# A planner with same-engine latencies, and attention scores on two 64-column array tiles, in a two-layer recurrent-attention kernel

## The chip, the cores and the metric

One core of a Trainium2 chip. The metric is the device time of one execution, in microseconds (us). Engines are named as in the profile: PE (TensorE matmuls), PEld (its weight loads), DVE (VectorE), ACT (ScalarE), POOL, SP.

## The reference, cut to what matters

Two equal layers, each recurrent memory attention followed by a gated feed-forward. Attention runs over 64 segments of 32 tokens; 8 memory rows go from each segment to the next, so a segment can't start before the one before it has gone through Wo.

```python
for s in range(n_seg):                      # 64 segments
    h = concat([mem, x[:, s*32:(s+1)*32]])  # 40 rows, 512 wide
    q, k, v = h@Wq, h@Wk, h@Wv              # 32 heads of 128
    p = softmax(where(mask, q@k.T * scale, -1e9))   # 40 x 40 per head
    o = (p@v) @ Wo
    mem = o[:, :8]; outs.append(o[:, 8:])
...
x = x + A(layernorm(x)); x = x + B(layernorm(x))    # layer 1
x = x + A(layernorm(x)); x = x + B(layernorm(x))    # layer 2
```

## The kernel before

Layer 2 runs six segments behind layer 1, so that a step (70 in all, 58 of them with both layers) handles one segment of each: 80 columns in place of 40. Layer 1 sits in partitions 0 to 39, layer 2 in 64 to 103. Nothing is issued where it is written: every piece of work goes to a planner as a task with an engine, an estimated duration and what it reads and writes. The planner (a list scheduler, longest remaining path first) fixes the order, which then stands in the program. The planner's numbers thus never are the time; they only decide the order.

```python
LAT = {"PE": 215.0, "DVE": 130.0, "ACT": 140.0, "POOL": 450.0, "SP": 2200.0}
...
for tk in reversed(T):                     # length of the remaining path
    m = 0.0
    for s in tk.succ:
        same = T[s].eng == tk.eng
        m = max(m, T[s].tail + (0.0 if same else tk.lat))   # same engine: no latency
    tk.tail = m + tk.dur + tk.boost
```

The score matmuls of a unit of three heads, and the softmax chain that follows each group of six heads:

```python
for i in range(nh):
    for idx, j in enumerate(jobs):         # j = layer; the unused half of lhsT holds zeros
        nc.tensor.matmul(s_all[:, uh - h0 + i, :], lhsT=qku[:, i, j, :],
                         rhs=qku[:, i, 2 + j, JOFF*j : JOFF*j + L],
                         start=(idx == 0), stop=(idx == len(jobs) - 1))
# ... then, per group:
# DVE  st = s_ps + mask          (L410)   reads the one score bank
# DVE  mx = max(st)              (L413)
# DVE  st = st - mx              (L415)
# ACT  st = exp(scale * st)      (L418)
# DVE  sm = sum(st)              (L420)
# DVE  rs = 1 / sm               (L422)
# DVE  pb = st * rs, per layer   (L426)   partitions 0.. and 64..
# PE   transpose pb into pt_ps   (L436)
```

Of the kernel before, what the change touches and what calls it, by code (L numbers as in the profile page):

```python
# [12 lines left out]
ALU = mybir.AluOpType  # L13
# [6 lines left out]
L = MEM + SEG  # L20
JOFF = 64
LW = JOFF + L
BLK = 4
EPS = 1e-5
# [16 lines left out]


class Task:
    __slots__ = ("eng", "dur", "lat", "fn", "deps", "succ", "tail", "boost", "ndep", "ready", "start", "idx", "on")

    def __init__(self, eng, dur, lat, fn, boost):
        self.eng, self.dur, self.lat, self.fn, self.boost = eng, dur, lat, fn, boost
        self.deps, self.succ = set(), []


class Planner:



    LAT = {"PE": 215.0, "DVE": 130.0, "ACT": 140.0, "POOL": 450.0, "SP": 2200.0}

    def __init__(self):
        self.tasks = []
# [3 lines left out]
    def add(self, eng, dur, fn, r=(), w=(), lat=None, boost=0.0):  # L62
        engs = eng if isinstance(eng, tuple) else (eng,)
        tk = Task(engs, dur, self.LAT[engs[0]] if lat is None else lat, fn, boost)
        tk.idx = len(self.tasks)
        for k in r:
            if k in self.writer:
                tk.deps.add(self.writer[k])
        for k in w:
            if k in self.writer:  # L70
                tk.deps.add(self.writer[k])
            for q in self.readers.get(k, ()):
                tk.deps.add(q)
        for k in w:
            self.writer[k] = tk.idx
            self.readers[k] = []
        for k in r:
            self.readers.setdefault(k, []).append(tk.idx)
        tk.deps.discard(tk.idx)
        self.tasks.append(tk)  # L80
        return tk

    def plan(self):
        T = self.tasks
        for tk in T:
            for d in tk.deps:
                T[d].succ.append(tk.idx)
        for tk in reversed(T):
            m = 0.0
            for s in tk.succ:  # L90
                same = T[s].eng == tk.eng
                m = max(m, T[s].tail + (0.0 if same else tk.lat))
            tk.tail = m + tk.dur + tk.boost
        free, avail = {"PE": 0.0, "ACT": 0.0}, {"PE": [], "ACT": []}
        for tk in T:
            tk.ndep = len(tk.deps)
            tk.ready = 0.0
            for e in tk.eng:
                free.setdefault(e, 0.0)
                avail.setdefault(e, [])  # L100
        waiting = {e: [] for e in free}
        ready = {e: [] for e in free}

        def release(tk):
            for e in tk.eng:
                heapq.heappush(waiting[e], (tk.ready, tk.idx))

        for tk in T:
            tk.on = None
            if tk.ndep == 0:  # L110
                release(tk)
        order = []
        left = len(T)
        while left:
            best = None
            for e in free:
                q, h = waiting[e], ready[e]
                while h and T[h[0][1]].on is not None:
                    heapq.heappop(h)
                while q and T[q[0][1]].on is not None:  # L120
                    heapq.heappop(q)
                if h:
                    t = free[e]
                elif q:
                    t = max(free[e], q[0][0])
                else:
                    continue
                if best is None or t < best[0]:
                    best = (t, e)
            t, e = best  # L130
            q, h = waiting[e], ready[e]
            while q and q[0][0] <= t:
                _, i = heapq.heappop(q)
                if T[i].on is None:
                    heapq.heappush(h, (-T[i].tail, i))
            while T[h[0][1]].on is not None:
                heapq.heappop(h)
            tk = T[heapq.heappop(h)[1]]
            tk.on, tk.start = e, t
            free[e] = t + tk.dur  # L140
            order.append(tk)
            left -= 1
            for s in tk.succ:
                n = T[s]
                same = n.eng == (e,)
                n.ready = max(n.ready, t + tk.dur + (0.0 if same else tk.lat))
                n.ndep -= 1
                if n.ndep == 0:
                    release(n)
        self.span = max(free.values())  # L150
        order.sort(key=lambda k: (k.start, k.idx))
        return order


class Kern:
# [149 lines left out]
    def layernorm_T(self, xb, xkey):  # L305
        nc, pl, D, DC = self.nc, self.pl, self.D, self.DC
        i = self.nxt("lns", 3)
        ln = self.lns[i]
        lk = ("lns", i)
        xi = self.nxt("xn", len(self.xn))  # L310
        xn = self.xn[xi]
        pl.add("DVE", dve_ns(D), lambda: nc.vector.bn_stats(out=ln[:, 0:6], in_=xb), r=[xkey], w=[lk])
        pl.add("DVE", 100, lambda: nc.vector.bn_aggr(out=ln[:, 6:8], in_=ln[:, 0:6]), w=[lk])
        pl.add("DVE", 80, lambda: nc.vector.tensor_scalar(out=ln[:, 8:9], in0=ln[:, 7:8], scalar1=EPS, scalar2=None, op0=ALU.add), w=[lk])
        pl.add("POOL", 500, lambda: nc.gpsimd.tensor_tensor(out=ln[:, 9:10], in0=ln[:, 8:9], in1=self.negh[:], op=ALU.pow), w=[lk], lat=100)
        pl.add("DVE", 80, lambda: nc.vector.scalar_tensor_tensor(out=ln[:, 10:11], in0=ln[:, 6:7], scalar=-1.0, in1=ln[:, 9:10],
                                                                  op0=ALU.mult, op1=ALU.mult), w=[lk])
        pl.add("ACT", act_ns(D) + 180, lambda: nc.scalar.activation(out=xn[:], in_=xb, func=ACTF.Identity, bias=ln[:, 10:11], scale=ln[:, 9:10]),
               r=[xkey, lk], w=[("xn", xi)])
        pst = self.misc[:, 0:(DC * P) // 2].bitcast(BF16).rearrange("p (c n) -> p c n", c=DC)  # L320

        def tr():
            for c in range(DC):
                nc.tensor.transpose(out=pst[:, c, :], in_=xn[:, c * P:(c + 1) * P], identity=self.ident[:])

        pl.add("PE", DC * mm_ns(P), tr, r=[("xn", xi)], w=["misc"])
        return pst
# [18 lines left out]
    def emit_step(self, t):  # L346
        nc, pl = self.nc, self.pl
        DC, H, LAG, R = self.DC, self.H, self.LAG, self.R
        jobs = tuple(j for j in (0, 1) if 0 <= t - j * LAG < self.NSEG)
# [15 lines left out]
        s_all = self.s_ps[:, 0:6 * L].rearrange("p (h k) -> p h k", h=6)  # L365
        pt_all = self.pt_ps[:, 0:6 * 2 * L].rearrange("p (h k) -> p h k", k=2 * L)

        for g, (h0, gsz, us) in enumerate(self.groups):
            hs = slice(0, gsz)
            for u in us:  # L370
                uh, nh = self.units[u]
# [3 lines left out]
                qku = self.qku[qi]  # L375

                def qk(uh=uh, nh=nh, pq=pq):
                    for i in range(nh):
# [10 lines left out]
                       w=[("pj", pji)])  # L389
# [10 lines left out]
                def sc(uh=uh, nh=nh, qku=qku, h0=h0):  # L400
                    for i in range(nh):
                        for idx, j in enumerate(jobs):
                            nc.tensor.matmul(s_all[:, uh - h0 + i, :], lhsT=qku[:, i, j, :], rhs=qku[:, i, 2 + j, JOFF * j:JOFF * j + L],  # L403
                                             start=(idx == 0), stop=(idx == len(jobs) - 1))

                pl.add("PE", nh * len(jobs) * mm_ns(L), sc, r=[("qku", qi)], w=["s_ps"])
            gi = self.nxt("st", 2)
            st, pb, mx, sm, rs = self.st[gi], self.pb[gi], self.mx[gi], self.sm[gi], self.rs[gi]
            n = gsz * L
            pl.add("DVE", dve_ns(n, True), lambda gsz=gsz, hs=hs, st=st: nc.vector.tensor_tensor(  # L410
                out=st[pr, hs], in0=s_all[pr, hs], in1=self.maskb[pr, :].unsqueeze(1).to_broadcast([npart, gsz, L]), op=ALU.add),
                r=["s_ps"], w=[("st", gi)])
            pl.add("DVE", dve_ns(n), lambda hs=hs, st=st, mx=mx: nc.vector.tensor_reduce(out=mx[pr, hs], in_=st[pr, hs], axis=AX.X, op=ALU.max),  # L413
                   r=[("st", gi)], w=[("mx", gi)])
            pl.add("DVE", dve_ns(n), lambda gsz=gsz, hs=hs, st=st, mx=mx: nc.vector.tensor_tensor(  # L415
                out=st[pr, hs], in0=st[pr, hs], in1=mx[pr, hs].unsqueeze(2).to_broadcast([npart, gsz, L]), op=ALU.subtract),
                r=[("mx", gi)], w=[("st", gi)])
            pl.add("ACT", act_ns(n), lambda hs=hs, st=st: nc.scalar.activation(out=st[pr, hs], in_=st[pr, hs], func=ACTF.Exp, scale=self.scale),  # L418
                   w=[("st", gi)])
            pl.add("DVE", dve_ns(n), lambda hs=hs, st=st, sm=sm: nc.vector.tensor_reduce(out=sm[pr, hs], in_=st[pr, hs], axis=AX.X, op=ALU.add),  # L420
                   r=[("st", gi)], w=[("sm", gi)])
            pl.add("DVE", 110, lambda hs=hs, rs=rs, sm=sm: nc.vector.reciprocal(out=rs[pr, hs], in_=sm[pr, hs]), r=[("sm", gi)], w=[("rs", gi)])  # L422
            for j in jobs:
# [3 lines left out]
                    out=pb[pj_, hs, JOFF * j:JOFF * j + L], in0=st[pj_, hs],  # L427
                    in1=rs[pj_, hs].unsqueeze(2).to_broadcast([npj_, gsz, L]), op=ALU.mult), r=[("st", gi), ("rs", gi)], w=[("pb", gi, j)])
# [14 lines left out]
            for n0 in range(0, H, 4):  # L443
# [5 lines left out]
                def vmm(pv=pv, n0=n0):  # L449
                    for c in range(DC):  # L450
# [5 lines left out]
                       r=[("pj", pji)], w=[("vsb", n0 // 4)])  # L456
# [38 lines left out]
        for idx, j in enumerate(jobs):  # L495
            s = t - j * LAG
            b = s // BLK
# [161 lines left out]
```

## Time and profile before

| | before |
|---|---|
| median of its first 3 runs | 2194.81 us |
| profiled span | 2196.4 us |
| matmuls, all with their own weight load | 42,116 |
| score matmuls (40 columns) | 4,096 |

The lines below are from the groups of instructions of the kernel before. The columns are: line, engine, operation, output and inputs, shape, count; then busy us and mean ns of one; then idle us of the engine just before them and what ended most of it.

```profile
L403 PE MATMUL s_ps<-qku 128*128 128x40 bf16 x4096 | 201.6, 180 | 24.5 <-DVE st L410 21.7
L403 PEld LDWEIGHTS <-qku 128*128 128x128 bf16 x4096 | 173.1, 96 | 78.6 <-issue 34.5
L436 PE MATMUL pt_ps<-ident,pb 128*128 128x80 bf16 (+1 forms) x2240 | 145.4, 198 | 32.8 <-DVE pb L426 27.8
```

A matmul's 180 ns here is a modelled life in a pipeline, not what it costs PE; the cost is how soon the next one starts, 25 ns. The last column shows where PE really stood still: at the scores until the bank was read, at the transposition until pb came.

### The profile page before, as it was taken

Reading aid. Unit: us, or ns where it says so; the run is one execution under the profiler, and the core shown is the slowest. Engines: PE = TensorE matmul, PEld = TensorE weight load, DVE = VectorE, ACT = ScalarE, POOL = GpSimd, SP = SyncE. Lnnn points to the kernel's source line nnn. Section 1 sums busy time; section 2 is a strip of 40 time slices with the busy share of each in tenths; the row PEclk is TensorE's granted clock in tenths of the full one; section 3 lists DMA queues with packets and bytes.
Section 4 is the critical chain, followed back from the end, with each engine's and each line's share of the span. In section 5 each row is a group of like instructions: output and inputs, shape, how many; then the busy total and the mean of one; then the engine's idle time right before and its main releaser. Section 6 shows DMA issues by size and latency. Waiting matters only on the chain.

```text
span 2196.4 us, 93329 instructions
## 1 busy us (share of the span) xinstructions
PE 2056.8 (94%) x42116; PEld 1742.8 (79%) x42116; DVE 1270.8 (58%) x3743; ACT 1299.0 (59%) x2919; POOL 43.5 (2%) x77
## 2 busy tenths in 40 slices
PE   4999999999999999999999999999999999999996
PEld 3777878788887878888787778878787888878775
DVE  4566566556646655665566466556655655565653
ACT  3556566565656656565666556566665666666552
POOL 1000000000000000000000000000000000000000
PEclk8999999999999999999999999999999999999997
DMA  9030223233232323324132332423233242324223
GB/s 333 29 89 17 77 60 108 74 108 103 75 108 60 108 74 108 103 75 122 55 113 60 108 103 74 119 58 109 63 113 98 83 116 60 115 58 126 70 61 107
DMA packets 317330, 203.17 MB, mean 92 GB/s; under 512 B 11770, under 2 KB 316930, under 8 KB 316930
## 3 DMA queue, kind: packets, MB, share of 16 engines
q1 hardware_dynamic: 316930, 197.19, 30.7%
q8 instruction: 329, 5.39, 1.0%
q14 instruction: 71, 0.58, 0.1%
HBM read 195.04 MB, written 2.10 MB: 90 GB/s over the span
## 4 chain that ended last, share of the span: by engine, by line
PE 62%; DVE 29%; issue 3%; ACT 3%; DMA 2%; POOL 0%; DVEq 0%; POOLq 0%; ACTq 0%
PE pj L385 22%; PE pj L451 16%; PE misc_ps L535 7%; PE wo_ps L477 7%; DVE pb L426 7%; DVE st L410 4%; DVE mx L413 3%; DVE st L415 3%; DVE sm L420 3%; PE misc_ps L556 3%; PE s_ps L403 3%; DVE ptsb L601 2%; DMA wd<-in_B_w_down_dram 2%; PE ot_ps L461 2%; PE pt_ps L436 2%
## 5 line engine op out<-in xcount | busy, mean ns | idle before, releaser
L385 PE MATMUL pj<-hT,wq_sb 128*128 128x80 bf16 (+1 forms) x8960 | 626.4, 198 | 16.1 <-DVE hT L488 13.6
L385 PE MATMUL pj<-hT,wk_sb 128*128 128x80 bf16 (+1 forms) x8960 | 627.6, 198 | 0.0
L451 PE MATMUL pj<-wv_sb,hT 128*104 128x512 bf16 x2240 | 568.3, 384 | 1.8 <-ACT vsb L599 1.6
L385 PEld LDWEIGHTS <-wq_sb 128*128 128x128 bf16 x8960 | 465.2, 99 | 59.6 <-issue 21.7
L599 ACT CAST qku<-pj 128x480 bf16<-128x480 f32 (+3 forms) x770 | 389.4, 514 | 144.4 <-PE pj L385 103.9
L599 ACT CAST vsb<-pj 104x512 bf16<-104x512 f32 (+2 forms) x560 | 326.1, 585 | 229.4 <-PE pj L451 223.4
L385 PEld LDWEIGHTS <-wk_sb 128*128 128x128 bf16 x8960 | 451.1, 99 | 0.0
L477 PE MATMUL wo_ps<-otsb,wo_sb 128*128 128x80 bf16 (+1 forms) x8960 | 389.3, 198 | 4.6 <-ACT otsb L599 4.2
L477 PEld LDWEIGHTS <-wo_sb 128*128 128x128 bf16 x8960 | 351.2, 99 | 40.7 <-issue 9.3
L451 PEld LDWEIGHTS <-hT 128*104 128x104 bf16 x2240 | 253.3, 128 | 128.1 <-issue 5.1
L410 DVE TENSOR_TENSOR st<-s_ps,maskb 104x240 f32<-104x240 f32 (+5 forms) x420 | 158.0, 376 | 296.7 <-PE s_ps L403 290.0
L426 DVE TENSOR_TENSOR pb<-st,rs 64x240 bf16<-64x240 f32 (+3 forms) x768 | 287.9, 375 | 26.7 <-DVE rs L422 0.5
L418 ACT ACTIVATE st<-st 104x240 f32<-104x240 f32 (+5 forms) x420 | 161.2, 384 | 188.2 <-DVE st L415 185.7
L599 ACT CAST otsb<-ot_ps 128x480 bf16<-128x480 f32 (+3 forms) x420 | 204.4, 487 | 66.6 <-PE ot_ps L461 60.4
L403 PEld LDWEIGHTS <-qku 128*128 128x128 bf16 x4096 | 173.1, 96 | 78.6 <-issue 34.5
L403 PE MATMUL s_ps<-qku 128*128 128x40 bf16 x4096 | 201.6, 180 | 24.5 <-DVE st L410 21.7
L544 DVE SCALAR_TENSOR_TENSOR hff<-th,misc_ps 128x256 bf16<-128x256 f32 x224 | 93.4, 417 | 210.6 <-ACT th L542 208.9
L420 DVE TENSOR_REDUCE sm<-st 104x6 f32<-104x240 f32 (+5 forms) x420 | 155.8, 371 | 95.7 <-ACT st L418 92.9
L535 PE MATMUL misc_ps<-xnT,wg 128*128 128x128 bf16 x1792 | 176.3, 222 | 9.5 <-DVE hff L544 6.6
L535 PE MATMUL misc_ps<-xnT,wu 128*128 128x128 bf16 x1792 | 176.6, 222 | 0.0
L436 PE MATMUL pt_ps<-ident,pb 128*128 128x80 bf16 (+1 forms) x2240 | 145.4, 198 | 32.8 <-DVE pb L426 27.8
L413 DVE TENSOR_REDUCE mx<-st 104x6 f32<-104x240 f32 (+5 forms) x420 | 156.9, 374 | 13.5
(52 smaller groups left out, 1671.3 us busy)
## 6 DMA issues: line engine op xcount, KB each, us to landing
wg<-in_B_w_gate_dram SPq DMA_DIRECT2D x224, 256.0 KB, 3.1
wu<-in_B_w_up_dram SPq DMA_DIRECT2D x224, 256.0 KB, 3.5
wd<-in_B_w_down_dram SPq DMA_DIRECT2D x224, 256.0 KB, 2.9
wv_sb<-in_A_Wv_dram SPq DMA_DIRECT2D x8, 512.0 KB, 9.6
wo_sb<-in_A_Wo_dram SPq DMA_DIRECT2D x8, 512.0 KB, 8.1
wq_sb<-in_A_Wq_dram SPq DMA_DIRECT2D x5, 768.0 KB, 10.3
wk_sb<-in_A_Wk_dram SPq DMA_DIRECT2D x5, 768.0 KB, 11.1
xs<-in_A_x_dram SPq DMA_DIRECT2D x16, 128.0 KB, 2.1
```

What stands on the lines that cost most here:

```text
L385: nc.tensor.matmul(o_ap, lhsT=W[:, c, h * P:(h + 1) * P], rhs=mv(c), start=(c == 0), stop=(c == DC - 1))
L403: nc.tensor.matmul(s_all[:, uh - h0 + i, :], lhsT=qku[:, i, j, :], rhs=qku[:, i, 2 + j, JOFF * j:JOFF * j + L], start=(idx == 0), stop=(id ...
L410: pl.add("DVE", dve_ns(n, True), lambda gsz=gsz, hs=hs, st=st: nc.vector.tensor_tensor(out=st[pr, hs], in0=s_all[pr, hs], in1=self.maskb[p ...
L413: pl.add("DVE", dve_ns(n), lambda hs=hs, st=st, mx=mx: nc.vector.tensor_reduce(out=mx[pr, hs], in_=st[pr, hs], axis=AX.X, op=ALU.max), r=[ ...
L418: pl.add("ACT", act_ns(n), lambda hs=hs, st=st: nc.scalar.activation(out=st[pr, hs], in_=st[pr, hs], func=ACTF.Exp, scale=self.scale), w=[ ...
L420: pl.add("DVE", dve_ns(n), lambda hs=hs, st=st, sm=sm: nc.vector.tensor_reduce(out=sm[pr, hs], in_=st[pr, hs], axis=AX.X, op=ALU.add), r=[ ...
L426: pl.add("DVE", dve_ns(n), lambda gsz=gsz, hs=hs, st=st, rs=rs, pb=pb, pj_=pj_, npj_=npj_, j=j: nc.vector.tensor_tensor(out=pb[pj_, hs, JO ...
L436: nc.tensor.matmul(o_ap, lhsT=pb[:, hl, :], rhs=idn, start=True, stop=True)
L451: nc.tensor.matmul(pv[0:LW, :], lhsT=hT[:, c, :], rhs=self.wv[:, c, n0 * P:(n0 + 4) * P], start=(c == 0), stop=(c == DC - 1))
L477: nc.tensor.matmul(self.wo_ps[:, c * ncol:(c + 1) * ncol], lhsT=self.wo[:, h, c * P:(c + 1) * P], rhs=otsb[:, hl, 0:ncol], start=(h == 0 a ...
L535: nc.tensor.matmul(gu[:, 2 * i + k, :], lhsT=W[:, c, i * P:(i + 1) * P], rhs=xnT[:, c, :], start=(c == 0), stop=(c == DC - 1))
L599: nc.scalar.copy(out=dst, in_=src)
```

## The change

Two parts. The **plan** now charges a latency between two tasks of DVE or of ACT where the second reads what the first has just written, and 45 ns more for any result that PE waits for; its other latencies between engines fall by 8 to 10 ns. The **scores** use one 64-column tile of the array per layer: columns 0 to 63 write partitions 0 to 63, columns 64 to 127 write 64 to 127, each a complete matmul without the zero half. The rest of the diff, cut here, marks which reads are of fresh results, uses `gap` at the second place where the planner had `same`, and plans 520 ns in place of 500 for POOL's one operation.

```diff
-    LAT = {"PE": 215.0, "DVE": 130.0, "ACT": 140.0, "POOL": 450.0, "SP": 2200.0}
+    LAT = {"PE": 205.0, "DVE": 122.0, "ACT": 130.0, "POOL": 100.0, "SP": 2200.0}
+    TO_PE = 45.0
...
+    def gap(self, a, b):
+        if a.eng == b.eng:
+            return a.lat if a.idx in b.fresh and a.eng[0] in ("DVE", "ACT") else 0.0
+        return a.lat + (self.TO_PE if b.eng[0] == "PE" else 0.0)
...
-                m = max(m, T[s].tail + (0.0 if same else tk.lat))
+                m = max(m, T[s].tail + self.gap(tk, T[s]))
...
-                            nc.tensor.matmul(s_all[:, uh - h0 + i, :], lhsT=qku[:, i, j, :], rhs=qku[:, i, 2 + j, JOFF * j:JOFF * j + L],
-                                             start=(idx == 0), stop=(idx == len(jobs) - 1))
+                            js = slice(JOFF * j, JOFF * j + JOFF)
+                            nc.tensor.matmul(s_all[js, uh - h0 + i, :], lhsT=qku[:, i, j, js], rhs=qku[:, i, 2 + j, JOFF * j:JOFF * j + L],
+                                             start=True, stop=True)
```

More of the change, by code (lines that the diff above doesn't have):

```diff
@@ L43 @@
 class Task:
-    __slots__ = ("eng", "dur", "lat", "fn", "deps", "succ", "tail", "boost", "ndep", "ready", "start", "idx", "on")
+    __slots__ = ("eng", "dur", "lat", "fn", "deps", "succ", "tail", "boost", "ndep", "ready", "start", "idx", "on", "fresh")
     def __init__(self, eng, dur, lat, fn, boost):
         self.eng, self.dur, self.lat, self.fn, self.boost = eng, dur, lat, fn, boost
-        self.deps, self.succ = set(), []
+        self.deps, self.succ, self.fresh = set(), [], set()
 class Planner:
-    LAT = {"PE": 215.0, "DVE": 130.0, "ACT": 140.0, "POOL": 450.0, "SP": 2200.0}
+    LAT = {"PE": 205.0, "DVE": 122.0, "ACT": 130.0, "POOL": 100.0, "SP": 2200.0}
+    TO_PE = 45.0
     def __init__(self):
@@ L68, in add @@
                 tk.deps.add(self.writer[k])
+                tk.fresh.add(self.writer[k])
         for k in w:
@@ L90, in plan @@
             for s in tk.succ:
-                same = T[s].eng == tk.eng
-                m = max(m, T[s].tail + (0.0 if same else tk.lat))
+                m = max(m, T[s].tail + self.gap(tk, T[s]))
             tk.tail = m + tk.dur + tk.boost
@@ L144, in plan @@
                 n = T[s]
-                same = n.eng == (e,)
-                n.ready = max(n.ready, t + tk.dur + (0.0 if same else tk.lat))
+                n.ready = max(n.ready, t + tk.dur + self.gap(tk, n))
                 n.ndep -= 1
@@ L312, in layernorm_T @@
         pl.add("DVE", dve_ns(D), lambda: nc.vector.bn_stats(out=ln[:, 0:6], in_=xb), r=[xkey], w=[lk])
-        pl.add("DVE", 100, lambda: nc.vector.bn_aggr(out=ln[:, 6:8], in_=ln[:, 0:6]), w=[lk])
-        pl.add("DVE", 80, lambda: nc.vector.tensor_scalar(out=ln[:, 8:9], in0=ln[:, 7:8], scalar1=EPS, scalar2=None, op0=ALU.add), w=[lk])
-        pl.add("POOL", 500, lambda: nc.gpsimd.tensor_tensor(out=ln[:, 9:10], in0=ln[:, 8:9], in1=self.negh[:], op=ALU.pow), w=[lk], lat=100)
+        pl.add("DVE", 100, lambda: nc.vector.bn_aggr(out=ln[:, 6:8], in_=ln[:, 0:6]), r=[lk], w=[lk])
+        pl.add("DVE", 80, lambda: nc.vector.tensor_scalar(out=ln[:, 8:9], in0=ln[:, 7:8], scalar1=EPS, scalar2=None, op0=ALU.add), r=[lk], w=[lk])
+        pl.add("POOL", 520, lambda: nc.gpsimd.tensor_tensor(out=ln[:, 9:10], in0=ln[:, 8:9], in1=self.negh[:], op=ALU.pow), r=[lk], w=[lk])
         pl.add("DVE", 80, lambda: nc.vector.scalar_tensor_tensor(out=ln[:, 10:11], in0=ln[:, 6:7], scalar=-1.0, in1=ln[:, 9:10],
-                                                                  op0=ALU.mult, op1=ALU.mult), w=[lk])
+                                                                  op0=ALU.mult, op1=ALU.mult), r=[lk], w=[lk])
         pl.add("ACT", act_ns(D) + 180, lambda: nc.scalar.activation(out=xn[:], in_=xb, func=ACTF.Identity, bias=ln[:, 10:11], scale=ln[:, 9:10]),
@@ L416, in emit_step @@
                 out=st[pr, hs], in0=st[pr, hs], in1=mx[pr, hs].unsqueeze(2).to_broadcast([npart, gsz, L]), op=ALU.subtract),
-                r=[("mx", gi)], w=[("st", gi)])
+                r=[("mx", gi), ("st", gi)], w=[("st", gi)])
             pl.add("ACT", act_ns(n), lambda hs=hs, st=st: nc.scalar.activation(out=st[pr, hs], in_=st[pr, hs], func=ACTF.Exp, scale=self.scale),
-                   w=[("st", gi)])
+                   r=[("st", gi)], w=[("st", gi)])
             pl.add("DVE", dve_ns(n), lambda hs=hs, st=st, sm=sm: nc.vector.tensor_reduce(out=sm[pr, hs], in_=st[pr, hs], axis=AX.X, op=ALU.add),
```

## The prediction

> **What bounds the kernel now.** I read the page first: busy shares, slices, chain. They name one engine.
>
> ```profile
> PE 2056.8 (94%) x42116; PEld 1742.8 (79%) x42116; DVE 1270.8 (58%) x3743; ACT 1299.0 (59%) x2919; POOL 43.5 (2%) x77
> ...
> PE   4999999999999999999999999999999999999996
> ...
> PEclk8999999999999999999999999999999999999997
> ...
> PE 62%; DVE 29%; issue 3%; ACT 3%; DMA 2%; POOL 0%; DVEq 0%; POOLq 0%; ACTq 0%
> ```
>
> PE is at 90% or more in every slice but the first and last, at a full clock; DVE and ACT are below 60%. But matmul ends are modelled, so 94% does not say that 94% is needed. For that I took the timeline of two short windows and read starts, not durations.
>
> ```profile
> 1001.68 0.31 PE L385 MATMUL pj<-hT,wk_sb 128*128 128x80 bf16 x4
> ...
> 1001.83 0.31 PE L403 MATMUL s_ps<-qku 128*128 128x40 bf16 x6
> ...
> 1001.98 0.30 PE L385 MATMUL pj<-hT,wq_sb 128*128 128x80 bf16 x4
> ...
> 1002.12 0.31 PE L385 MATMUL pj<-hT,wk_sb 128*128 128x80 bf16 x4
> ```
>
> Four 80-column matmuls go by in 0.144 us (36 ns each), six 40-column score matmuls in 0.150 us (25 ns each). Over all individual starts the medians are 36 ns (80 columns), 25 (40), 56 (128) and 216 (512). Counts by shape from the groups of instructions: 25,984 x 35.6 + 9,472 x 25 + 3,968 x 55.6 + 2,688 x 215.6 ns = 926 + 237 + 221 + 580 = 1,963 us of pure streaming. The span is 2,196, so 233 us (10.6%) is not streaming: 9 before the first matmul, 4 after the last one starts, and 215 in spacings longer than the shape needs, of which 194 lie in 400 spacings that are late by 100 ns or more. About 60 of the total sit in the first and last 100 us; between, it is a steady 7 to 8 us in every 100. The waits name who makes PE late:
>
> ```profile
> PE pt_ps L436 <- DVE pb L426: 27.8, 41, 2.9
> ...
> PE s_ps L403 <- DVE st L410: 21.7, 32, 1.1
> ...
> PE misc_ps L324 <- ACT xn L318: 19.3, 17, 3.4
> ...
> PE pj L385 <- DVE hT L488: 13.6, 43, 0.3
> ```
>
> The softmax chain on DVE ends late for the transposition (L436), the score bank is still being read when the next group's scores want it (L403), and each step's first projection waits for the memory rows of the step before (L385). These are waits that a static order can hide or fail to hide. The order is made by a planner in the kernel, and its picture of DVE is wrong here:
>
> ```profile
> 1000.28 0.41 DVE L410 TENSOR_TENSOR st<-s_ps,maskb 104x240 f32<-104x240 f32 x1 [0.51 <-PE s_ps L403]
> ...
> 1000.72 0.40 DVE L413 TENSOR_REDUCE mx<-st 104x6 f32<-104x240 f32 x1
> ...
> 1001.15 0.41 DVE L415 TENSOR_TENSOR st<-st,mx 104x240 f32<-104x240 f32 x1
> ```
>
> Each of these needs the one before it, and they start 0.43 to 0.44 us apart. Where the next DVE instruction is independent (L413 followed by another group's L420) the median spacing is 0.319. The planner before charges 320 ns and nothing for the dependence.
>
> **What the Trainium skill says.** (1) "TensorE: Matmul & The Clock Gate", Part 1: matmuls start N/2.4 + about 2.5 ns apart, never under about 25 ns. The trace agrees: 36, 56, 216 and 25 ns. So the score matmuls stand on a floor, and fewer rows or columns of weights alone make none faster. (2) "TensorEngine Tiling (Array Packing)", Restrictions and Key Properties: column tiling switches fast weight load off, and changing the tiling mode, not just the tile, drains the engine. The kernel before is untiled all through, so its trace shows no drain. It does show a load that is not a full 128 columns wide: V loads 104 columns, and its second matmul starts 236 ns after the first, not 216, when 40-column matmuls went before, 231 after 80-column ones. Such a load takes about 25 + 20 = 45 to 36 + 15 = 51 ns. (3) "TensorE: Matmul & The Clock Gate", Part 3: matmuls on different tiles overlap, about 4 ns apart in start; no run here shows it. (4) "VectorE: DVE Perf Modes", Two Vector instructions with no wait between them: an instruction whose operands start in another quadrant than the last is held. The trace agrees: the two pb writes (L426, partitions 0 and 64) are independent, yet 414 ns apart. Neither planner knows this.
>
> **The change, part by part.**
>
> *The plan.* Nothing is added or removed on any engine: the counts of matmuls by kind are equal, so the 1,963 us stay. What moves is the order. I built both and measured, in streaming time on PE, how much other work the order puts between a producer and its consumer, and compared it with the time the consumer needs. The need is set so that the shortfalls of the kernel before add up to the stall its trace shows there; the same need then goes over the new order.
>
> - Scores to transposition (420 groups): need 3.39 us, stall 49 us. The lowest 5% of distances rises from 2.60 to 3.24: shortfall left 25. Gain 24. This is the 4 x 122 ns of dependence now in the plan, plus 45 to PE.
> - Scores to the next group's scores: need 1.24, stall 35; lowest 5% from 0.88 to 1.10, lowest 10% from 0.88 to 1.32: 7 left. Gain 27.
> - Step to step (69): need 0.50, stall 24; the median filler goes from 0.04 to 0.47: 14 left. Gain 10.
> - Last down-projection to the next transposition (16): need 5.2, filler 4.18 to 4.61: gain 6.
> - PV to Wo: need 0.69, the lowest 5% falls from 0.46 to 0.33: loss 9. PV to PV, transposition to PV and gate-up to gate-up: losses of 5, 2 and 1.
> - Q/K to scores: the low tail shortens (lowest 5% 1.94 to 1.52). Its need cannot be told from the bank's; the cast takes about 1.0 to 1.1 us with its waits, and few lie under that: loss 0 to 10.
>
> Sum: 67 gained, 17 to 27 lost, about 45 us off (2.0%). Shortfalls at several edges overlap, and a new order makes new waits, so I take 10 to 80.
>
> *The score tiles.* 4,096 matmuls and 4,096 loads stay; loads go from 128 fast columns to 64 slow ones. Scaled from V: 64/104 x (45 to 51) = 28 to 31 ns, an estimate. If loads run one behind another, each score matmul takes 28 to 31 in place of 25: +12 to +25 us. If the two layers' tiles truly overlap, a pair takes about 30 in place of 50: 1,856 pairs x 20 = 37 us saved. Entry and exit: in the new order the score matmuls stand in 501 unbroken blocks (624 before), so 1,002 mode changes. A drain in the skill's sense costs at least the 128 rows (53 ns at 2.4 GHz, an estimate from the array in "TensorE: Matmul & The Clock Gate") plus a load that can no longer be hidden (about 30): 1,002 x 85 ns = +85 us, all on PE, none beside anything. Zero padding: the removed half of the weights was multiplied anyway, so no time in it. Dropping the accumulation across layers saves no instruction.
>
> **The rivals.**
>
> 1. *Tiles are nearly free, the plan decides.* For: V shows a slow load in the middle of fast ones with a delay of 15 to 20 ns and no drain. 2,195 - 45 + 5 = 2,155; 2,110 with a good plan and overlapping tiles. I give it 0.55.
> 2. *Each mode change drains.* For: the skill says so. The plan's gain is eaten: 2,195 - 45 + 85 = 2,235. 0.35.
> 3. *The drain is the whole matmul latency* (the records put a 40-column matmul at 179 ns, modelled). 1,002 x 150 ns = +150: 2,300. 0.10.
> 4. *The plan only moves waits.* DVE holds (414 ns pairs) and bank waits stay unmodelled, and the gain falls to 10. That adds 35 to any of the above. DVE as the new bound I rule out at 58% busy; weight DMA, at 3 us to landing and 31% share, too.
>
> **Range and chances.** The median of the mixture lies between rivals 1 and 2, nearer to 1: 2,170 us. Low end 2,110 (rival 1 with everything well), high end 2,255 (rival 2 with a weak plan). Faster by 2% means under 2,151: a little over half of rival 1, 0.36. Slower means over 2,239: rival 3, and a good third of rival 2 less its better plans, 0.20. Within 2%: 0.44.
>
> **What would show it right or wrong.** Plan: the waits of L436-to-pb and L403-to-st (now L443 and L410) should fall together by half, those of Wo on otsb rise by some us. Tiles: the start-to-start spacing inside score blocks (25 now) should be 28 to 31 if loads bound it, about 15 if pairs overlap; the spacing from the last matmul before a score block to its first, and from its last to the next kind, should show 0 or 50 and more beyond the shape's own time, with nothing waited for. A drain near 150 ns, or score spacings of 50 ns, would prove me wrong upward; plan waits that fall to nothing would, downward.

## The result, and the profile after

| | before | after |
|---|---|---|
| median | 2194.74 us (4 runs) | 2168.38 us (4 runs) |
| lowest to highest | 2193.3 to 2200.37 | 2167.15 to 2169.21 |
| profiled span | 2196.4 us | 2167.4 us |

The ratio is 0.9875, with a 95% interval of 0.9857 to 0.9893: the same within 2%, 26 us faster. A ratio here is always the mean time of one kernel's fast runs over that of the other's fast runs of the same rounds, so not quite the ratio of the medians beside it. The kernel before is run anew with each set of rounds; its medians were 2194.7 to 2197.8 us, so kernels of different sets are best compared by their ratios.

These are the lines of the page of the changed kernel that answer to the first ones shown of before: busy time, PE by slices, its clock, the chain that ended last by engine.

```profile
PE 2091.9 (97%) x42006; PEld 1751.3 (81%) x42116; DVE 1204.5 (56%) x3702; ACT 1307.1 (60%) x2960; POOL 43.7 (2%) x77
...
PE   5999999999999999999999999999999999999996
...
PEclk8999999999999999999999999999999999999997
...
PE 92%; DVE 3%; ACT 2%; issue 1%; DMA 1%; another core or an unknown queue 0%; SPq 0%; POOLq 0%; ACTq 0%; DVEq 0%
```

The chain has changed its nature: DVE held 29% of it and holds 3%. PE is busier by 35 us in a span shorter by 29. (110 matmul records are missing from this trace.) The waits of the changed kernel that answer to those of before (columns: who waited for whom, us in total, times, longest us):

```profile
PE pt_ps L443 <- DVE pb L433: 11.6, 7, 2.9
...
PE misc_ps L330 <- ACT xn L324: 7.7, 4, 3.4
...
PE pj L391 <- DVE hT L495: 5.3, 17, 0.3
```

Seven waits for pb in place of 41, and the scores' wait for the bank is not in the list any more. The four waits shown of before sum to 82 us, and these to 25: 58 us less idle PE at four places alone, yet the span fell by 29 only. Where the rest went is seen in the timeline. This is a place in the changed kernel where four score matmuls (two heads, both layers) stand between two blocks of twelve Wo matmuls (columns: start us, us, engine, line, operation, count):

```profile
1007.02 0.59 PE L484 MATMUL wo_ps<-otsb,wo_sb 128*128 128x80 bf16 x12
1007.55 0.24 PE L410 MATMUL s_ps<-qku 128*64 128x40 bf16 x4
1007.72 0.60 PE L484 MATMUL wo_ps<-otsb,wo_sb 128*128 128x80 bf16 x12
```

Read the starts. Twelve Wo matmuls stream in 12 x 36 ns = 0.43 us, but the scores start 0.53 us after the first: 0.10 lost before the block. The four scores then last until 1007.72, 0.17 us, where four at 25 ns need 0.10. PE counts as busy all through, since the modelled ends of its matmuls reach over the hole. The individual starts of the whole trace say it exactly:

| spacing, ns (median) | before | after |
|---|---|---|
| last 80-column matmul to first score | 36 | 132 |
| last 128-column matmul to first score | 56 | 149 |
| last 512-column matmul to first score | 216 | 309 |
| last 40-column matmul of another kind to first score | 25 | 109 |
| last score to the next kind | 25 | 118 |
| inside a block, both layers | 25 each | pairs 3 to 4 apart; second pair 53 after the first, then one pair every 32 |
| inside a block, one layer only | 25 each | 31 to 32 each after the first two |

So going into a block costs 93 to 96 ns beyond the shape's own time (84 after a 40-column matmul, 51 of the 501 blocks), and going out 93 more. Inside a block two matmuls take 32 ns, so 16 each: the prediction had named "about 15 if pairs overlap".

### The profile page after: what moved, and what is told of

Read it like the earlier page. It is cut to its first block, busy times and chain, and to the rows that moved or that the text cites. A ratio compares the mean times of both kernels' runs of the same rounds, so it can differ in the third digit from the quotient of the medians.

```text
span 2167.4 us, 93419 instructions
## 1 busy us (share of the span) xinstructions
PE 2091.9 (97%) x42006; PEld 1751.3 (81%) x42116; DVE 1204.5 (56%) x3702; ACT 1307.1 (60%) x2960; POOL 43.7 (2%) x77
## 4 chain that ended last, share of the span: by engine, by line
PE 92%; DVE 3%; ACT 2%; issue 1%; DMA 1%; another core or an unknown queue 0%; SPq 0%; POOLq 0%; ACTq 0%; DVEq 0%
PE pj L391 28%; PE pj L458 23%; PE wo_ps L484 13%; PE misc_ps L542 10%; PE s_ps L410 6%; PE pt_ps L443 4%; PE ot_ps L468 3%; PE misc_ps L563 3%; DMA wd<-in_B_w_down_dram 1%; PE misc_ps L330 1%; ACT ptsb L606 1%; ACT otsb L606 1%; DVE sm L427 1%; ACT st L425 0%
## 5 line engine op out<-in xcount | busy, mean ns | idle before, releaser
L391 PEld LDWEIGHTS <-wq_sb 128*128 128x128 bf16 x8960 | 471.3, 99 | 71.6 <-issue 13.8
L606 ACT CAST qku<-pj 128x480 bf16<-128x480 f32 (+3 forms) x770 | 380.7, 514 | 208.0 <-PE pj L391 177.3
L484 PE MATMUL wo_ps<-otsb,wo_sb 128*128 128x80 bf16 (+1 forms) x8960 | 397.7, 198 | 10.7 <-ACT otsb L606 9.6
L606 ACT CAST ptsb<-pt_ps 128x480 bf16<-128x480 f32 (+3 forms) x291 | 138.2, 475 | 82.5 <-PE pt_ps L443 78.8
L422 DVE TENSOR_TENSOR st<-st,mx 104x240 f32<-104x240 f32 (+5 forms) x420 | 158.3, 377 | 9.6
L410 PE MATMUL s_ps<-qku 128*64 128x40 bf16 x4096 | 160.9, 191 | 0.9 <-ACT qku L606 0.7
```

Of the source, the lines that this page charges most:

```text
L391: nc.tensor.matmul(o_ap, lhsT=W[:, c, h * P:(h + 1) * P], rhs=mv(c), start=(c == 0), stop=(c == DC - 1))
L410: nc.tensor.matmul(s_all[js, uh - h0 + i, :], lhsT=qku[:, i, j, js], rhs=qku[:, i, 2 + j, JOFF * j:JOFF * j + L], start=True, stop=True)
L422: pl.add("DVE", dve_ns(n), lambda gsz=gsz, hs=hs, st=st, mx=mx: nc.vector.tensor_tensor(out=st[pr, hs], in0=st[pr, hs], in1=mx[pr, hs].uns ...
L484: nc.tensor.matmul(self.wo_ps[:, c * ncol:(c + 1) * ncol], lhsT=self.wo[:, h, c * P:(c + 1) * P], rhs=otsb[:, hl, 0:ncol], start=(h == 0 a ...
L606: nc.scalar.copy(out=dst, in_=src)
```

## The experiments

The two parts of the change are independent: the planner never looks at what a task issues. The order of all instructions in e1 is that of the changed kernel, and in e2 that of the kernel before; the traces agree: the same operations in the same order on DVE, ACT and POOL, and on PE but for the missing records. There were twelve runs, in three sets, of ten different kernels, and all gave correct results.

### The plan alone, the tiles alone (e1, e2)

**e1_plan_only** is the changed kernel with the score matmuls put back:

```diff
-                            js = slice(JOFF * j, JOFF * j + JOFF)
-                            nc.tensor.matmul(s_all[js, ...], lhsT=qku[:, i, j, js], ..., start=True, stop=True)
+                            nc.tensor.matmul(s_all[:, ...], lhsT=qku[:, i, j, :], ..., start=(idx == 0), stop=(idx == len(jobs) - 1))
```

> The new plan with the score matmuls of the kernel before (untiled, zero padded); the order on every engine is that of the changed kernel. Theory A (from the changed kernel's trace): the tiles cost PE about 72 us net (501 blocks x about 190 ns of entry and exit, less about 18 ns per pair), so the plan alone is worth about 98 us: 2,085 to 2,125 us, some of the waits coming back that the mode changes had covered. Theory B (the prediction's own sum): the plan is worth 45 us and the tiles cost about 20: 2,140 to 2,160 us.

Measured: 2103.42 us, ratio 0.9574 (0.9558 to 0.959). Theory A holds, and the prediction's sum (B) falls. The same place in the program in e1's timeline:

```profile
1005.37 0.59 PE L483 MATMUL wo_ps<-otsb,wo_sb 128*128 128x80 bf16 x12
1005.79 0.26 PE L409 MATMUL s_ps<-qku 128*128 128x40 bf16 x4
1005.90 0.59 PE L483 MATMUL wo_ps<-otsb,wo_sb 128*128 128x80 bf16 x12
```

From Wo to the scores 0.42 us, where it was 0.53; the scores 0.11, where they were 0.17. And e1's waits are about those of the changed kernel (the first two lines are busy time and the chain that ended last):

```profile
PE 2026.0 (96%) x42116; PEld 1734.5 (83%) x42116; DVE 1196.4 (57%) x3702; ACT 1302.9 (62%) x2960; POOL 43.7 (2%) x77
...
PE 86%; DVE 8%; ACT 3%; issue 1%; DMA 1%; POOL 0%; ACTq 0%; POOLq 0%; DVEq 0%
...
PE pt_ps L442 <- DVE pb L432: 12.4, 7, 2.9
...
PE misc_ps L330 <- ACT xn L324: 10.5, 17, 3.4
```

So the lost holes did not merely hide waits: without them, nearly the same few waits remain.

**e2_tiles_only** is the kernel before with the tiled score matmuls (e1's edit the other way round).

> The order of the kernel before with the tiled score matmuls. Theory A: 624 score blocks x about 190 ns = 119 us, less 1,856 pairs x 18 ns = 33 us: 86 us more PE time, of which up to 30 may fall into waits that PE has anyway (35 us of waiting at score blocks): 2,250 to 2,285 us. Rival: the mode changes fall mostly into time in which PE would have waited, and the tiles alone cost under 25 us: 2,195 to 2,220 us.

Measured: 2252.66 us, ratio 1.0253 (1.0238 to 1.0269). Theory A holds, at its lower end. Its timeline, at a block of twelve scores between gate-up and Q/K matmuls:

```profile
1000.26 0.39 PE L536 MATMUL misc_ps<-xnT,wu 128*128 128x128 bf16 x4
1000.58 0.37 PE L404 MATMUL s_ps<-qku 128*64 128x40 bf16 x12
1000.88 0.32 PE L385 MATMUL pj<-hT,wq_sb 128*128 128x80 bf16 x4
```

Four matmuls of 56 ns need 0.22 us, and 0.32 go by: the same 0.10 on the way in. Twelve scores with the way out take 0.30 us, just what twelve untiled ones take at 25 ns. All that the overlap of the two tiles saves goes on the way out, and the way in is pure loss.

The four corners, in ratio to the kernel before:

| | old plan | new plan |
|---|---|---|
| untiled | 1 | 0.9574 |
| tiled | 1.0253 | 0.9875 |

The plan gives 93 us; the tiles take 56 us in the old order and 65 us in the new. The old order has more blocks (624 x 186 ns = 116 us of holes, some 24 saved inside), so about 36 us of its loss fell into time in which PE would have waited anyway; in the new order hardly any did.

### Which number of the plan does it (e3, e4, e8, e9)

**e3_fresh_only** has the cross-engine numbers of before (its same-engine latencies, which the planner takes from the same table, are thus 130 and 140 ns and not 122 and 130); **e4_to_pe_only** has no same-engine latency. Both are e1 with one edit:

```diff
 # e3
-    LAT = {"PE": 205.0, "DVE": 122.0, "ACT": 130.0, ...}
-    TO_PE = 45.0
+    LAT = {"PE": 215.0, "DVE": 130.0, "ACT": 140.0, ...}
+    TO_PE = 0.0
 # e4
-            return a.lat if a.idx in b.fresh and a.eng[0] in ("DVE", "ACT") else 0.0
+            return 0.0
```

> Untiled, and of the plan only the same-engine latency for a read of a fresh result on DVE and ACT; the cross-engine numbers stay as before. Theory A1: that latency is what the old plan lacked (four dependent DVE steps of 117 ns each in every softmax chain), so this alone gives most of the plan's gain: within 25 us of e1. Rival A2: the 45 ns towards PE count as much, and this gives half or less of the gain: 2,140 us or more.

Measured: 2109.89 us, ratio 0.9605 (0.959 to 0.9619): 87 of the 93 us. Theory A1 holds.

> Untiled, and of the plan only the changed cross-engine numbers and the 45 ns towards PE, without the same-engine latency. Theory A1: a small gain, 0 to 30 us below the kernel before: 2,165 to 2,195 us. Rival A2: half or more of the plan's gain: 2,150 us or less.

Measured: 2183.74 us, ratio 0.9941 (0.9926 to 0.9956): 13 us. A1 holds here too. Almost all of the plan's gain is the one line on fresh results of the same engine.

Is 122 ns right because it is the measured number, or is any room good? **e8_half_lat** and **e9_double_lat** scale it (`return 0.5 * a.lat if ...`, `return 2.0 * a.lat if ...`).

> Untiled, the new plan with half of the same-engine latency (61 and 65 ns). Theory A1 (the plan is good because the number is the measured one): between none (e4, 2,184) and full (e1, 2,103), nearer to the middle: 2,125 to 2,160 us. Rival A2 (any sign of dependence is enough): within 10 us of e1. Rival A3 (orders of such a planner scatter by some tens of us whatever the number): anything, in no order with e4, e1 and the double.

> Untiled, the new plan with twice the same-engine latency (244 and 260 ns). Theory A1 (the measured number is the right one, and more is only padding): no better than e1, 2,100 to 2,125 us. Rival: the more room for dependences, the better, as waits are what costs: 2,095 us or less.

| same-engine latency in the plan | median us | ratio to before |
|---|---|---|
| none (e4) | 2183.74 | 0.9941 |
| half (e8) | 2119.93 | 0.9653 |
| as measured (e1) | 2103.42 | 0.9574 |
| double (e9) | 2090.24 | 0.9514 |

Both of my A1 expectations fell. Half gave 2,120, below the range that A1 set, though not within 10 us of e1 as A2 had it: already most of the gain. Double gave 2,090, below A1's range and within the rival's: the measured number is not the optimum, more room is better here. The sequence is ordered, which speaks against mere scatter of orders (A3), but each step is one order only. Why room beyond the measured latency pays is open. A list plan reckons every duration as certain, and waits it doesn't know of come on top, so slack may be an insurance; that is an argument and no run here shows it. Where it pays can be read: of spacings late by 100 ns or more, e1 has 22 us before transpositions and 18 before Wo, e9 13 and 5; against that, the step's first projections lose 13 more. e9 beats both kernels by more than any other run.

### Is it the change of mode? (e6)

**e6_more_changes** leaves the middle head of each unit of three untiled, in the changed kernel:

```diff
                     for i in range(nh):
                         for idx, j in enumerate(jobs):
+                            if i == 1:
+                                nc.tensor.matmul(s_all[:, ...], lhsT=qku[:, i, j, :], ..., start=(idx == 0), stop=(idx == len(jobs) - 1))
+                                continue
                             js = slice(JOFF * j, JOFF * j + JOFF)
```

> The changed kernel with the middle head of each unit of three untiled again (zero padded), so that such a unit goes tiled, untiled, tiled: 700 units with two more mode changes each. Theory A: a change of tile mode costs about 93 ns one way and 90 to 118 the other, wherever it stands: 700 x 187 = 131 us more, plus about 10 for the untiled pairs: 2,290 to 2,315 us. Rival: the 93 and 118 ns belong to the edge of a score block (its wait for the cast of Q and K, or weights that cannot be fetched ahead of that wait), not to the mode: 2,175 to 2,195 us.

Measured: 2324.43 us, ratio 1.0588 (1.0572 to 1.0604): 156 us more than the changed kernel, 223 ns for each of the 700 units. That is 9 us above theory A's range and 129 above the rival's, so A's mechanism is the one that fits, and its size was short. Over the whole trace a turn from tiled to untiled scores takes 139 ns from start to start and a turn back 109, where untiled scores are 25 apart. One merged block of two units in its timeline (L414 tiled, L410 untiled):

```profile
999.60 0.21 PE L414 MATMUL s_ps<-qku 128*64 128x40 bf16 x2
999.75 0.22 PE L410 MATMUL s_ps<-qku 128*128 128x40 bf16 x2
999.89 0.24 PE L414 MATMUL s_ps<-qku 128*64 128x40 bf16 x4
1000.07 0.22 PE L410 MATMUL s_ps<-qku 128*128 128x40 bf16 x2
1000.22 0.21 PE L414 MATMUL s_ps<-qku 128*64 128x40 bf16 x2
1000.36 0.39 PE L447 MATMUL pt_ps<-ident,pb 128*128 128x80 bf16 x6
```

All twelve matmuls read one kind of operand from one kind of buffer; within a unit there is nothing new to wait for, and still each turn from one mode to the other leaves a hole: five stretches of two or four small matmuls take 0.14 to 0.18 us each. From the first tiled block to the transpositions it is 0.76 us; twelve untiled scores are 0.30. The cost goes with the mode, wherever the edge stands. What it consists of, work that must end first or weights that can't be loaded ahead across the change, no run here tells apart.

### Do the two tiles overlap? (e5)

**e5_pairs_apart** orders the scores of a unit by layer, then head:

```diff
-                    for i in range(nh):
-                        for idx, j in enumerate(jobs):
+                    for idx, j in enumerate(jobs):
+                        for i in range(nh):
```

> The changed kernel with the score matmuls of a unit ordered by layer, then head, so that neighbours in the stream are in the same tile and not in two. Theory A: two neighbours 4 ns apart is real overlap of the two tiles, and a tile that is loaded again and again is bound by its 28 ns load: a unit of 3 pairs then takes about 165 ns in place of 89 within the block; 1,856 pairs x 24 ns = 45 us more, of which some falls into waits: 2,195 to 2,215 us. Rival: the 4 ns is only how the profile records two matmuls, and the time is the same within 5 us of 2,168.

Measured: 2171.33 us, ratio 0.9893 (0.9878 to 0.9907). The intervals of e5 and of the changed kernel meet, so the times are the same as far as these runs tell. The total is what the rival said, and theory A's 45 us are not there. But the rival's reason doesn't fit either, for the starts did change: neighbours are now 10 and 22 ns apart, not 4 and 28, at the same 32 ns for two. With one layer only, where all matmuls go to one tile, it is 31 to 32 ns for one. Two tiles do twice the work of one in the same time, in both orders. The reading that fits all three is that each tile works through its own matmuls, and the stream runs ahead of both: the second tile's first matmul is then one pair of instructions behind (4 ns) when the layers alternate, and three pairs behind (10 ns) when they don't. The records do not name the tile, so this reading is argued, not shown. What is shown is that the overlap does not hang on the two tiles alternating in the stream.

### The slow load by itself (e7, e12, beside e11), and a last plan (e10)

The prediction took the price of a load that is not 128 columns wide from V's matmuls. **e7_v128** and **e12_v128_again** are e1 with V's stationary operand padded from 104 to 128 columns; **e11_plan_again** is e1 once more, in the set of e12.

```diff
-        self.hT = [c.tile([P, DC, LW], BF16, ...)]
+        self.hT = [c.tile([P, DC, P], BF16, ...)]
...
-                        nc.tensor.matmul(pv[0:LW, :], lhsT=hT[:, c, :], ...
+                        nc.tensor.matmul(pv[:, :], lhsT=hT[:, c, :], ...
```

> The untiled kernel with the new plan (e1), and V's stationary operand padded from 104 to 128 columns with the zeros that its buffer gets at the start. Theory: the 15 to 20 ns by which the second V matmul comes late behind 40- or 80-column matmuls is the slow load of a block that is not 128 columns wide; padded, they go: about 6 us off, 2,095 to 2,100 us. Rival: the delay is the turn from short to long matmuls and stays; 2,102 to 2,106 us.

Measured: 2100.75 us, ratio 0.9571 (0.9557 to 0.9586), against 0.9574 for e1 in another set: too near to tell. It lies just above the theory's range and just below the rival's.

> e1 once more, as the measure for e10 and e12 on the same chip: 2,101 to 2,106 us, 0.957 of the kernel before.

Measured: 2104.35 us, ratio 0.9576 (0.9561 to 0.959), as expected.

> e7 once more beside e1, to tell 3 us from nothing. Theory: 2 to 6 us below e11 (its trace lost the 15 to 20 ns behind short matmuls, but part of that falls into waits). Rival: the same within 1 us.

Measured: 2099.17 us, ratio 0.9555 (0.9541 to 0.9569): 5 us below e11 by the medians, as the theory said. The runs do not overlap (e11's lowest was 2101.88, e12's highest 2100.17), though the intervals of their ratios do. The spacing is clear: in e1 the second V matmul comes 231 ns after the first behind 80-column matmuls and 236 behind 40-column ones; padded, 218 and 215 (medians over the V blocks of e7's trace whose records are complete). In the timeline of e1, then of e7, eight V matmuls behind 80-column ones:

```profile
1003.62 1.91 PE L457 MATMUL pj<-wv_sb,hT 128*104 128x512 bf16 x8
1005.37 0.59 PE L483 MATMUL wo_ps<-otsb,wo_sb 128*128 128x80 bf16 x12
```

```profile
1001.37 1.89 PE L457 MATMUL pj<-wv_sb,hT 128*128 128x512 bf16 x8
1003.10 0.59 PE L483 MATMUL wo_ps<-otsb,wo_sb 128*128 128x80 bf16 x12
```

1.75 us against 1.73. A narrower load is the slower one, and it has no hole of 93 ns at its edges: those come with the tile mode, not with the slow load.

**e10_held** is e7 with 100 ns more in the plan for each of the two pb writes:

```diff
-                pl.add("DVE", dve_ns(n), lambda gsz=gsz, hs=hs, st=st, rs=rs, pb=pb, ...
+                pl.add("DVE", dve_ns(n) + (100.0 if both else 0.0), lambda gsz=gsz, hs=hs, st=st, rs=rs, pb=pb, ...
```

> e7 (untiled, new plan, V padded to 128 columns) with 100 ns more in the plan for each pb write of a two-layer step, since those start about 110 ns later than independent DVE work does (414 against 310 to 325 ns). Theory: the plan then knows the last unmodelled link of the softmax chain, and the waits of the transposition on pb shrink: 2,080 to 2,098 us. Rival: what is left of the waits is not from this chain, and the new order is only another one: 2,095 to 2,115 us.

Measured: 2097.77 us, ratio 0.9545 (0.9531 to 0.956). That lies in both theories' ranges, and only 1.4 us below e12: inconclusive by the time. The traces say more. Late spacings (100 ns or more) before transpositions went from 45 in e12, 22.8 us, to 16, 18.9 us; those before Wo rose from 17.9 to 29.6 us, and the sum over all kinds stayed at 103. The plan did relieve this link, and the new order waited elsewhere.

## Why the prediction was right, and wrong

The time was right: 2,170 predicted, 2,168 measured, and "the same" was the likeliest class. Its parts were not. Its middle amounts to 45 us off for the plan and some 20 on for the tiles; 93 and 65 were measured. Both terms were too small, by 48 and by 45 us, and cancelled. That the total came out to 2 us is luck. (Its sums hold but for small ones: "a little over half of rival 1" is 0.36 of 0.55, and with every spacing counted the late ones are 227 us, not 215.)

**"All on PE, none beside anything": right.** PE is the bound, the 1,963 us of streaming stay but for the scores, and DVE and the weight DMA did not become the bound.

**The plan: the mechanism right, the term mis-sized.** The step "Sum: 67 gained, 17 to 27 lost, about 45 us off" should have read 93; even "10 to 80" did not hold it. By the prediction's own edges, stall in us (the columns add up to the spacings late by 100 ns or more, 194 before and 101 in e1):

| edge | before | predicted after | e1 |
|---|---|---|---|
| scores to transposition | 49 | 25 | 22 |
| scores to the next group's scores | 35 | 7 | 1 |
| step to step | 24 | 14 | 15 |
| PV to Wo | 10 | 19 | 18 |
| last down-projection to transposition | 15 | 9 | 0 |
| transposition to PV | 13 | 15 | 12 |
| gate-up to gate-up | 14 | 15 | 7 |
| waits at none of these edges | 34 | not counted | 26 |

The big edges came out within a few us, the one loss of weight (PV to Wo) too. The method, distance in the order against the time needed, is sound. What failed was the ledger. The loss of "0 to 10" at Q/K to scores was no loss: those stalls are the same ones as those of the score bank. PV to PV and transposition to PV end at the same matmul, and the loss was booked at both; neither came, nor did that at gate-up. Eight us of waits at no edge of my list went away too, where I had let them stand, the down-projection's gain was 15, not 6, and the bank's 34, not 27. In full, and with every late spacing counted however small, stall fell from 227 to 133 us, by 94, and the span by 95.

**The rivals: the weights were wrong.** "Tiles are nearly free, the plan decides" had 0.55 and fell. Its reason, V's slow load "with a delay of 15 to 20 ns and no drain", was true of V and did not carry over, as V is not in another tile mode; e6 and e7 show the two costs apart. "Each mode change drains" had 0.35 and was the true one. Its size, 85 ns a change, was near: 93 measured. Its total of 2,235 was wrong by the plan's missing 48 us, and by the overlap, which it left out.

**The score tiles, step by step.** 1,002 changes x 93 ns = 93 us; by the traces of e1 and the changed kernel, whose orders are equal, the ways in take 47 us more and the ways out 47. Inside the blocks, the 3,595 recorded spacings from score to score take 67.7 us where they take 93.1 in e1, so 25 saved; the prediction had 37, since it did not know that the second pair starts 53 ns after the first. "28 to 31 ns" for a slow load: 31 to 32. Sum 68 us; 65 are measured between e1 and the changed kernel, so about 3 fell into time in which PE would have waited.

**"The plan only moves waits": wrong.** They went, and the chain of waits went from 62% PE to 86% in e1 (92% in the changed kernel, holes counted in).

## What to carry to other kernels

When a change has two parts, run each alone before believing the sum: here 93 us of gain and 65 of loss looked like a change of little worth, and undoing half of it was the better kernel. Array tiling costs by the block and saves by the matmul: at 186 ns for going in and out, and 9 ns saved per matmul of a pair, a block needs over twenty score matmuls to break even (an estimate from these figures; no block was that long), and these have 2 to 12. In a static plan, a dependence between two instructions of one engine is a latency like any other, and a little too much of it did no harm here; a busy share that rises is no sign of a good change, as the tiles raised PE's from 96% to 97% with holes.

## What the Trainium skill lacked or had wrong

- "TensorEngine Tiling (Array Packing)", Key Properties, says that a change of tiling mode drains the engine, but gives no cost. Here, between 128x128 and 128x64: 84 to 96 ns on the way in and 93 on the way out, beyond the spacing that the shapes need.
- "TensorE: Matmul & The Clock Gate": Part 3 measures the overlap of tiles at 512 columns only. At 40 columns two column tiles give two matmuls with their loads per 32 ns, against 50 untiled and 31 to 32 for one matmul where a single tile is used. The page's section on LDWEIGHTS has columns / 1.2 in ns, which is 87 ns for 104 columns and 53 for 64; V's 104-column loads hold up the next matmul as a load of 45 to 51 ns would (an estimate from its spacings), and 64-column loads in a single tile follow one another at 31 to 32 ns. Its Back-to-back issue gap has about 81 ns for a load and a matmul at 128 columns; here such pairs start 56 ns apart.
- "VectorE: DVE Perf Modes", The DRAIN you can't avoid, excepts an instruction that is not held, but gives no figure for what that saves. Here 240-element instructions start 0.43 to 0.44 us apart where the second reads the first's result, and about 0.32 (0.31 to 0.33 by the pair) where it doesn't, so about 117 ns are to be had by putting independent work between. The section on instructions with no wait between them gives no price for a held one: the second pb write comes 414 ns after the first, some 95 late, and an independent instruction after it, back at partition 0, comes 436 to 437 after that by the median.
